# Three edits to the planned order of an attention and feed-forward kernel: a later load, six small transfers on another queue, exponentials ahead of casts

## The chip, the cores and the metric

The kernel runs on one core of one Trainium2 chip. The metric is the device time of one execution in microseconds; the median of three runs before the change is 892.74 us (892.28 to 894.45). The engines are TensorE (PE; its weight loads are listed as PEld), VectorE (DVE), ScalarE (ACT), GpSimd (POOL) and SyncE (SP), which here issues transfers only. Each works through its own instructions in order and waits on semaphores for the others. Transfers are issued from the queue of SyncE or of ScalarE.

## The reference, cut to what matters

Attention with a block mask over 4 batches x 8 heads, 768 positions, 64 dimensions a head, in float32, and then a feed-forward layer with the activation h - tanh(h):

```python
scores = q @ k.T / sqrt(64)                    # per batch and head, 768 x 768
scores = where(mask, scores, -1e9)             # blocks of 32: window, border, sampled
attn = exp(scores - scores.max(-1)); attn /= attn.sum(-1) + 1e-9
x = (attn @ v)                                 # heads side by side: 3072 tokens x 512
h = x @ w_in                                   # 512 -> 2048
out = (h - tanh(h)) @ w_out                    # 2048 -> 512
```

## The kernel before, in words

Heads are taken in 16 pairs. For a pair, `x` (its keys and queries, 768 KB), and `v` are loaded; VectorE splits `x` into high words and low rests in three pieces (`mask_words` into a PSUM bank, `low_words` into the tile `lo`), and SyncE copies high and low parts into one of three *slots*, from which TensorE reads its operands. A slot also holds 24 rows that add the mask, and one row, the 89th, that holds for each query the negated maximum of its scores.

That row is made per head `h` well ahead of use. TensorE computes the 88-row product (`smax`), VectorE takes maxima out of PSUM (`most`, tile `mc`), joins them (`most_join`, tile `mj`), TensorE turns them (`most_turn`), VectorE negates them into the tile `nm` (`most_send`), and a transfer of 3 KB puts `nm` into the slot's row 88. All matmuls of that head's scores (89 rows) wait for this transfer.

The scores are worked off in 96 *units* `n` (two key blocks of 128 rows, three units a head), each in three pieces of 512 columns, one PSUM bank each. `scores` fills the bank on TensorE, `exps` takes the exponential on ScalarE into the tile `pe`, `high` casts it to 16 bits in two halves (`ph`, ScalarE), `low` subtracts (`pl`, GpSimd up to unit 89), and `accum` multiplies both with the split `v` (tile `vhl`) on TensorE, 36 small matmuls a unit, into two banks of their own. The other six banks go round among scores, maxima and the small things by a counter (`bank`). Once in a pair ScalarE also casts `v` (`v_parts`, one or two instructions), in the first four pairs GpSimd subtracts for it too. In `low` and `v_parts` a name such as `pl` or `vhl` in a row of the profile is the tile written.

What sets the order is a list: `at(time, function, ...)` puts each step at a planned time, in units of half an attention unit (unit `n` stands at 2n), the list is sorted and every engine keeps that order. `smt(n)` is the planned time of unit n's maxima, 12 to 16 ahead of its scores. `LATE` shifts, for pairs 2 to 6, the load of `x`, its splitting and its copies to the slot (three numbers a pair). The loads of weights for the feed-forward part and its first conversions run within the attention; the feed-forward layer follows from about 350 us, on the same list. Since each recorded operation goes through one helper, nearly all rows of the profile bear its line, L91, and are told apart by tile names.

Of the kernel before, what the change touches and what calls it, by code (L numbers as in the profile page):

```python
# [64 lines left out]
TAIL, LASTN = 90, 93  # L65
SPIN = (-40, 14), (-1.95, 6), (-0.2, 2), (3.1, 3), (3.5, 1)
RAMP, NRAMP = 4, 24
LATE = {2: (10, 10, 6), 3: (8, 9, 3), 4: (5, 8, 2), 5: (2, 4, 1), 6: (1, 2, 0.5)}

THR2 = 0.16  # L70
C3 = -0.01988785306343693
# [33 lines left out]
@with_exitstack  # L105
def attention_ffn(ctx, tc, kq, v, samp, w_in, w_out, blocks, out):
    nc = tc.nc
    cst = ctx.enter_context(tc.tile_pool(name="cst", bufs=1))
    dpool = ctx.enter_context(tc.tile_pool(name="dpool", bufs=1, space=DRAM))
    xscr = [dpool.tile([P, T, DM], F32, name=f"xscr{b}") for b in range(B)]  # L110

    ident = cst.tile([P, P], F32, name="ident")
    make_identity(nc, ident)
    bias = [cst.tile([P, 1], F32, name=f"bias{i}") for i in range(2)]
    for x, val in zip(bias, (QB, THR2)):
        nc.vector.memset(x, val)

    slots = [cst.tile([P, 4, 2, S], F32R, name=f"slot{i}") for i in range(NSLOT)]
    wt = {(m, ft): dpool.tile([P, 512], F32, name=f"w{m}{ft}") for ft in range(NPRE) for m in "io"}
    part = [dpool.tile([P, DM], F32, name=f"part{j}") for j in range(CT)]  # L120
    f2 = ctx.enter_context(tc.tile_pool(name="f2", bufs=2))
    px = ctx.enter_context(tc.tile_pool(name="px", bufs=2))
    ffn = FFN(tc, w_in, w_out, xscr, ident, bias, slots, wt, out, f2, part, px)
    psum = ctx.enter_context(tc.tile_pool(name="psum", bufs=1, space=PSUM))
    banks = [psum.tile([P, 512], F32, name=f"ps{i}") for i in range(8)]
    ffn.banks, ffn.hb, ffn.cv, ffn.xt = banks[:4], banks[4:6], banks[6], banks[7]
    with ExitStack() as actx:
        turn = iter(range(10**6))
        ps = lambda n=6: banks[next(turn) % n], banks[6:]
        ffn.nc = InOrder(tc)  # L130
        attention(actx, tc, kq, v, samp, w_in, w_out, blocks, xscr, ident, ps, slots, wt, px, f2, ffn)
        ffn.nc = InOrder(tc, InOrder.ENGINES[:4])
    with ExitStack() as fctx:
        ffn.rest(fctx)


def attention(ctx, tc, kq, v, samp, w_in, w_out, blocks, xscr, ident, ps, slots, wt, px, f2, ffn):
    nc = InOrder(tc)
# [164 lines left out]
    mcs, sms = {}, {}  # L303
# [30 lines left out]
    def most_send(h):  # L334
        pr, j = divmod(h, 2)
        nm = p2.tile([T, P], F32R, tag="nm", name=f"nm{h}")
        nc.vector.tensor_scalar(out=nm, in0=mcs.pop(h), scalar1=-1.0, scalar2=8.0 * PBITS * math.log(2.0), op0=ALU.mult, op1=ALU.add)
        nc.sync.dma_start(
            out=sB[pr % NSLOT].bitcast(F32)[88:89, j, :].rearrange("o (t c) -> o t c", t=T), in_=nm.bitcast(F32)
        )  # L340

# [72 lines left out]
    def at(time, f, *args):  # L414
        ev.append((time, len(ev), f, args))
# [19 lines left out]
    for pr in range(NPAIR):  # L435
        t0 = 12 * pr
        late = LATE.get(pr, (0, 0, 0))
        at(t0 - 34.2 + late[0] if pr > 1 else -26.6 if pr else -49, load_x, pr)
# [27 lines left out]
    def smt(n):  # L466
        return 2 * n - LEAD + RAMP * max(0, 1 - n / NRAMP)

    for h in range(2 * NPAIR):
        t0 = smt(3 * h + 2)  # L470
        late = 0 if h < 4 else 0.8
        at(t0 + (2.65 if h > 4 else 1.6), most_join, h)
        at(t0 + 2.5 + late, most_turn, h)
        at(t0 + 2.75 + late, most_send, h)
        for step in range(3):
            at(6 * h + 10.3 + 0.5 * step, norm, h, step)
    for n in range(6 * NPAIR):
        for x in range(3):
            at(2 * n + 0.45 * x, scores, n, x)
            at(smt(n) + 0.45 * x + 0.25, smax, n, x)  # L480
            if n < 3:
                at(smt(n) + 0.45 * x + 0.26, spin, 1)
            at(smt(n) + 0.45 * x + 0.6, most, n, x)
            at(2 * n + 0.45 * x + 0.4, exps, n, x)
        at(2 * n + 1, high, n, 0)
        at(2 * n + 1.6, high, n, 1)
        at(2 * n + 1.7, low, n)
        at(2 * n + LAV, accum, n)
# [367 lines left out]
```

## Time and profile before

| | before |
|---|---|
| median of three runs | 892.74 us (892.28 to 894.45) |
| the profiled execution's own time | 895.38 us |
| its span, first to last instruction | 893.6 us |
| mean granted TensorE clock | 0.998 |
| TensorE busy | 875.4 us (98%) |
| VectorE busy | 717.8 us (80%) |
| ScalarE busy | 648.6 us (73%) |
| GpSimd busy | 505.8 us (57%) |

All durations come from the one profiled execution, so sums are made against its 895.38 us, which are 2.64 us above the median of the runs; 1.8 us of them lie outside the span. A row of a timeline gives start, duration, engine, line, operation, tile written <- tiles read, shapes and count, and in brackets the idle time before it and who ended that. A row of a stage gives the stretch, its length, the busy time of PE, PEld, DVE, ACT and POOL with their counts, the granted TensorE clock (1.00 is full), the share of time the 16 DMA engines were busy, and GB/s. TensorE's busy time is modelled for pipelined matmuls and can hide waits of some 0.1 us.

### The profile page before, as it was taken

The numbers are of one execution on the slowest core, as the hardware profiler recorded it, in microseconds if no ns is written. First come the engines' busy times: TensorE is split into PE (matmuls) and PEld (weight loads), VectorE is DVE, ScalarE is ACT, GpSimd is POOL, SyncE is SP. The second block draws the span as 40 slices with busy tenths as digits, with TensorE's granted clock in tenths as the row PEclk, the third lists the DMA queues.
The fourth block names the chain that finished last, engine by engine and source line by source line (L and its number), as shares of the span: only waits on it lengthen the run. The fifth ranks groups of instructions, "written<-read, shape, count | busy, mean of one in ns | idle before, by whom it ended". The sixth has DMA issues, their size and how long they took to land.

```text
span 893.6 us, 18523 instructions
## 1 busy us (share of the span) xinstructions
PE 875.4 (98%) x7078; PEld 734.8 (82%) x7078; DVE 717.8 (80%) x1262; ACT 648.6 (73%) x1080; POOL 505.8 (57%) x266
## 2 busy tenths in 40 slices
PE   7899999999999999999999999999999999999997
PEld 6778878888888888878888888888888888888885
DVE  8888899999999988998997687676668666866664
ACT  5799989999999999777776655565556555555553
POOL 7788989999999995677775222222222222222222
PEclk9999999999999999999999999999999999999999
DMA  6787788887888865347420202120102010001001
GB/s 182 191 212 182 182 218 206 204 210 193 211 214 222 199 173 175 117 142 225 140 76 34 63 7 66 30 34 15 47 5 34 10 47 1 1 1 48 0 1 47
DMA packets 87316, 97.53 MB, mean 109 GB/s; under 512 B 41764, under 2 KB 62436, under 8 KB 87228
## 3 DMA queue, kind: packets, MB, share of 16 engines
q1 hardware_dynamic: 86764, 95.31, 40.9%
q10 hardware_dynamic: 464, 1.05, 0.5%
q8 instruction: 55, 0.90, 0.4%
q14 instruction: 33, 0.27, 0.1%
HBM read 44.64 MB, written 15.20 MB: 67 GB/s over the span
## 4 chain that ended last, share of the span: by engine, by line
PE 80%; DVE 10%; DMA 5%; issue 2%; ACT 2%; POOL 1%; SPq 1%; ACTq 0%; DVEq 0%; POOLq 0%
PE ps L91 80%; DVE mc L91 4%; DVE ps L91 2%; DMA rawx<-kq 1%; DMA slot<-nm 1%; DVE lo L91 1%; DMA stage<-w_out 1%; DMA slot<-rawx 1%; ACT pe L91 1%; DMA rawv<-v 1%; SPq L91 1%; ACT ph L91 1%; DVE xq L91 1%; DVE pl L91 1%; DVE cvti L91 0%
## 5 line engine op out<-in xcount | busy, mean ns | idle before, releaser
L91 POOL TENSOR_TENSOR pl<-pe,ph 128x1536 f16<-128x1536 f32 x90 | 287.2, 3206 | 33.6 <-ACT ph L91 22.0
L91 POOL TENSOR_TENSOR gl<-t,gh 128x512 fp32r<-128x512 f32 x96 | 125.0, 1302 | 309.0 <-ACT gh L91 293.0
L91 PE MATMUL ps<-slot 128*128 128x512 f32 (+5 forms) x1224 | 257.7, 355 | 9.0 <-DMA slot<-nm 2.2
L91 PEld LDWEIGHTS ps<-slot 128*128 128x128 f32 (+2 forms) x1224 | 186.8, 191 | 38.0 <-DVE mc L91 4.1
L91 DVE TENSOR_REDUCE mc<-ps 128x1 f32<-128x512 f32 (+1 forms) x288 | 192.4, 680 | 21.4 <-PE ps L91 20.0
L91 ACT ACTIVATE u<-ps 128x512 f32<-128x512 f32 x96 | 57.4, 598 | 197.7 <-PE ps L91 197.7
L91 ACT ACTIVATE pe<-ps 128x512 f32<-128x512 f32 x288 | 164.0, 586 | 17.6 <-PE ps L91 14.4
L91 PE MATMUL ps<-slot,wx 128*128 128x512 f32 x720 | 173.0, 389 | 0.0
L91 ACT ACTIVATE ph<-pe 128x768 f16<-128x768 f32 x187 | 157.6, 843 | 5.4
L91 PEld LDWEIGHTS ps<-slot,wx 128*128 128x128 f32 x720 | 135.2, 188 | 28.0
L91 PE MATMUL ps<-wx,gh 128*128 128x512 f32 x480 | 147.9, 389 | 0.0
L91 PEld LDWEIGHTS <-ph 128*128 128x128 f16 x2304 | 112.6, 97 | 16.1 <-issue 13.1
L91 DVE TENSOR_TENSOR t<-t,ps 128x512 f32<-128x512 f32 x74 | 50.7, 685 | 88.1 <-ACT t L91 88.1
L91 PE MATMUL ps<-vhl,ph 128*128 128x65 f16 (+1 forms) x2304 | 120.6, 195 | 0.0
L91 PE MATMUL ps<-vhl,pl 128*128 128x65 f16 x1152 | 116.3, 193 | 0.6 <-DVE pl L91 0.3
L91 PEld LDWEIGHTS <-pl 128*128 128x128 f16 x1152 | 107.2, 100 | 1.0 <-POOL pl L91 0.6
L91 PEld LDWEIGHTS ps<-wx,gh 128*128 128x128 f32 x480 | 90.1, 188 | 18.5
L91 PE MATMUL ps<-wx,gl 128*128 128x512 f32 x240 | 93.5, 389 | 0.0
L91 DVE COPY_PREDICATED t<-mk,ps 128x512 f32<-128x512 int32 x96 | 71.3, 743 | 6.7 <-ACT mk L91 0.4
L91 DVE TENSOR_TENSOR ps<-ps,u 128x512 f32<-128x512 f32 x96 | 66.6, 694 | 11.5 <-ACT hs L91 11.4
L91 DVE SCALAR_TENSOR_TENSOR ps<-qq,ps 128x512 f32<-128x512 f32 x96 | 66.6, 694 | 8.0 <-DVE ps L91 0.5
L91 PE MATMUL ps<-slot,slot 128*128 128x512 f32 x288 | 69.6, 391 | 0.6 <-DVE t L91 0.6
(103 smaller groups left out, 1186.6 us busy)
## 6 DMA issues: line engine op xcount, KB each, us to landing
slot<-rawx SPq DMA_DIRECT2D x31, 384.0 KB, 7.1
slot<-lo SPq DMA_DIRECT2D x62, 192.0 KB, 3.1
slot<-rawx SPq DMA_DIRECT2D x61, 192.0 KB, 4.1
rawx<-kq SPq DMA_DIRECT2D x15, 768.0 KB, 6.1
stage<-w_in SPq DMA_DIRECT2D x13, 512.0 KB, 3.8
stage<-w_out SPq DMA_DIRECT2D x13, 512.0 KB, 4.0
rawv<-v SPq DMA_DIRECT2D x16, 384.0 KB, 5.3
xscr<-xq SPq DMA_DIRECT2D x16, 384.0 KB, 3.6
```

The costliest lines, as they stand in the source:

```text
L91: r = f(*args, **kw)
```

## The change

Three things move; nothing is computed differently.

The load of the third pair's `x` is planned 4.2 later (from -0.2 to 4.0) and its splitting 3 later. The 3 KB transfer of `nm` becomes a step of its own, `most_dma`; for the first six heads it is issued from ScalarE's queue, planned 0.3 after the negation, for the others from SyncE's as before. And for units 8 to 89 the first cast is planned at 2n + 1.35 instead of 2n + 1, which is after the third exponential (2n + 1.3).

```diff
-LATE = {2: (10, 10, 6), 3: (8, 9, 3), 4: (5, 8, 2), 5: (2, 4, 1), 6: (1, 2, 0.5)}
+APART = 8
+EARLYH = 6
+LATE = {2: (14.2, 13, 6), 3: (8, 9, 3), 4: (5, 8, 2), 5: (2, 4, 1), 6: (1, 2, 0.5)}
...
         nc.vector.tensor_scalar(out=nm, in0=mcs.pop(h), scalar1=-1.0, scalar2=8.0 * PBITS * math.log(2.0), op0=ALU.mult, op1=ALU.add)
-        nc.sync.dma_start(
+        mcs[h] = nm
+
+    def most_dma(h):
+        pr, j = divmod(h, 2)
+        nm = mcs.pop(h)
+        (nc.scalar if h < EARLYH else nc.sync).dma_start(
             out=sB[pr % NSLOT].bitcast(F32)[88:89, j, :].rearrange("o (t c) -> o t c", t=T), in_=nm.bitcast(F32)
         )
...
         at(t0 + 2.75 + late, most_send, h)
+        at(t0 + 2.75 + late + (0.3 if h < EARLYH else 0), most_dma, h)
...
-        at(2 * n + 1, high, n, 0)
+        at(2 * n + (1.35 if APART <= n < TAIL else 1), high, n, 0)
```

On ScalarE, from the last exponential of unit 1 into unit 2 (`pe1` is unit 1's exponentials, `ph1` its casts, `ps3` bank 3, the number behind `_` a running one), before:

```order
L91 ACTIVATE pe1_294<-ps3_98 128x512
L91 ACTIVATE ph1_309<-pe1_294 128x768
L91 ACTIVATE pe2_336<-ps2_97 128x512
L91 ACTIVATE pe2_336<-ps4_99 128x512
L91 ACTIVATE ph2_348<-pe2_336 128x768
L91 ACTIVATE pe2_336<-ps0_95 128x512
```

and now:

```order
L93 ACTIVATE pe1_292<-ps3_98 128x512
L93 ACTIVATE ph1_307<-pe1_292 128x768
L93 DMA slot0_73<-nm1_326 1x6x128
L93 ACTIVATE pe2_336<-ps2_97 128x512
L93 ACTIVATE pe2_336<-ps4_99 128x512
L93 ACTIVATE ph2_346<-pe2_336 128x768
L93 ACTIVATE pe2_336<-ps5_100 128x512
```

Head 1's transfer stands between unit 1's second cast and unit 2's first exponential, and unit 2's third exponential reads bank 5 instead of bank 0.

On ScalarE, units 9 and 10, with the two casts of the third pair's `v` (`rawv2`, `vhl2`) between, before:

```order
L91 ACTIVATE pe9_827<-ps1_96 128x512
L91 ACTIVATE pe9_827<-ps3_98 128x512
L91 ACTIVATE ph9_842<-pe9_827 128x768
L91 ACTIVATE pe9_827<-ps5_100 128x512
L91 ACTIVATE rawv2_474<-rawv2_474,sb2_812 128x768
L91 ACTIVATE vhl2_111<-rawv2_474 128x12x64
L91 ACTIVATE ph9_842<-pe9_827 128x768
```

and now:

```order
L93 ACTIVATE pe9_827<-ps1_96 128x512
L93 ACTIVATE pe9_827<-ps3_98 128x512
L93 ACTIVATE pe9_827<-ps5_100 128x512
L93 ACTIVATE ph9_883<-pe9_827 128x768
L93 ACTIVATE rawv2_472<-rawv2_472,sb2_812 128x768
L93 ACTIVATE vhl2_111<-rawv2_472 128x12x64
L93 ACTIVATE ph9_883<-pe9_827 128x768
```

The first cast went behind the third exponential; the casts of `v` still stand ahead of the second cast.

On SyncE, from the copies of the second pair's `x` on (`rawx1`, `rawv1` and `lo1` are of the second pair, `rawx2` of the third), before:

```order
L91 DMA slot1_74<-rawx1_173 64x768 x2
L91 DMA rawx2_245<-kq 128x1536
L91 DMA rawv1_270<-v 128x768
L91 DMA slot1_74<-rawx1_173 64x768 x2
L91 DMA slot1_74<-lo1_265 64x768
L91 DMA slot0_73<-nm1_328 1x6x128
L91 DMA slot1_74<-lo1_265 64x768 x3
L91 DMA rawv2_474<-v 128x768
L91 DMA slot2_75<-rawx2_245 64x2x768
L91 DMA slot1_74<-nm2_526 1x6x128
L91 DMA rawx3_538<-kq 128x1536
```

and now:

```order
L93 DMA slot1_74<-rawx1_173 64x768 x2
L93 DMA rawv1_268<-v 128x768
L93 DMA slot1_74<-rawx1_173 64x768 x2
L93 DMA slot1_74<-lo1_263 64x768
L93 DMA rawx2_328<-kq 128x1536
L93 DMA slot1_74<-lo1_263 64x768 x3
L93 DMA rawv2_472<-v 128x768
L93 DMA slot2_75<-rawx2_328 64x2x768
L93 DMA rawx3_536<-kq 128x1536
```

The third pair's `x` went behind the first low part of the second pair, the transfers of `nm1` and `nm2` are gone from this queue, and the load of the fourth pair's `x` follows the third pair's copy at once.

## The prediction, made before the changed kernel was run

> **What bounds the kernel now.** I read the page first, then the granted clock by stage, then TensorE's idle time and what ended it, then the queues that end it. The page:
>
> ```profile
> PE 875.4 (98%) x7078; PEld 734.8 (82%) x7078; DVE 717.8 (80%) x1262; ACT 648.6 (73%) x1080; POOL 505.8 (57%) x266
> ```
>
> TensorE is the bound, so only time in which it idles or runs slowly can be won. By stage (busy time of each engine, granted clock, DMA share):
>
> ```profile
> 29.89:33.30 3.41, 1.80 (x11) 1.29 (x10) 2.94 (x5) 0.59 (x3) 3.10 (x1) 1.00 1.04 235
> 33.30:36.71 3.41, 3.41 (x42) 2.89 (x41) 1.38 (x3) 2.71 (x5) 0.56 (x1) 0.50 0.78 171
> 36.71:40.12 3.41, 3.41 (x50) 3.02 (x49) 3.25 (x8) 2.46 (x5) 2.56 (x1) 1.00 0.00 0
> ```
> ```profile
> 200.00:250.00 50.00, 49.85 (x690) 43.10 (x689) 47.71 (x105) 48.45 (x75) 46.71 (x16) 1.00 0.80 206
> ```
>
> In the steady attention (200 to 250 us) TensorE idles 0.15 of 50 us: nothing to win, though ScalarE (48.45) and GpSimd (46.71) are nearly full too. The early stretch is different: of 3.41 us TensorE idles 1.6, and in the next 3.41 us it is granted half its clock, worth 3.41 x 0.5 = 1.7 us. TensorE's rows name the stall:
>
> ```profile
> 17.43 0.50 PE L91 MATMUL ps<-slot 89*128 89x512 f32 x1
> ...
> 27.70 0.95 PE L91 MATMUL ps<-slot 128*128 128x512 f32 x3 [0.91 <-DVE mc L91]
> ...
> 29.61 0.94 PE L91 MATMUL ps<-slot 88*128 88x256 f32 x4
> 32.16 2.02 PE L91 MATMUL ps<-slot 89*128 89x512 f32 x8 [1.61 <-DMA slot<-nm]
> ...
> 67.57 1.92 PE L91 MATMUL ps<-slot 89*128 89x512 f32 x9 [0.57 <-DMA slot<-nm]
> ```
>
> The 89-row matmul reads the row of negated maxima, so it waits until that 3 KB transfer lands. The chain of waits gives issue and flight:
>
> ```profile
> 27.08 5.04 DMA slot<-nm
> ```
> ```profile
> 61.53 6.00 DMA slot<-nm
> ```
>
> Head 0's transfer was fast: SyncE issued it at 15.46 and the matmul that needs it ran at 17.43, at most 1.97 us.
>
> ```profile
> 15.46 0.80 SPq L91 DMA_DIRECT2D slot<-nm x1
> ```
>
> So 5.04 and 6.00 us are about 2 us of transfer and 3 to 4 us behind the bulk loads on SyncE's queue (DMA share 1.04 in the row of 29.89 us).
>
> **The change, part by part.** (1) *Head 1's maxima on ScalarE's queue.* They are ready when VectorE's row ends, 26.78 + 0.27 = 27.05:
>
> ```profile
> 26.78 0.27 DVE L91 TENSOR_SCALAR nm<-ps 6x128 fp32r<-6x128 f32 x1
> 26.98 0.67 DVE L91 TENSOR_REDUCE mc<-ps 128x2 f32<-128x512 f32 x1
> ```
>
> In the new order the transfer stands between units 1 and 2 on ScalarE. Before, ScalarE ran there:
>
> ```profile
> 26.34 1.09 ACT L91 ACTIVATE pe<-ps 128x512 f32<-128x512 f32 x2
> ...
> 28.46 0.60 ACT L91 ACTIVATE pe<-ps 128x512 f32<-128x512 f32 x1 [0.17 <-PE ps L91]
> 29.09 0.84 ACT L91 ACTIVATE ph<-pe 128x768 f16<-128x768 f32 x1
> 32.75 1.08 ACT L91 ACTIVATE pe<-ps 128x512 f32<-128x512 f32 x2 [2.81 <-PE ps L91]
> ```
>
> ScalarE will wait for 27.05 and issue; taking 0.75 us per issue (head 0's issue is 0.80) it goes on at 27.83, 1.49 late. Behind it in its queue stand unit 2's exponentials and casts: 27.83 + (29.09 - 26.34 - 0.17) + 0.75 = 31.16 is when unit 3's first exponential can start, against 32.75 before. That is a gain of 1.6 on ScalarE's side; the 1.49 are covered by its 2.81 us of idle time.
>
> TensorE's side: the third x's first mask tile no longer takes a PSUM bank, so unit 2's third score tile moves from bank 0 (read by the maximum that ends at 26.98 + 0.67 = 27.65, the 0.91 us wait) to bank 5, free at 27.05. TensorE's work from 27.70 to 30.55 (29.61 + 0.94) then starts at about 27.1 and ends at 29.95. The transfer lands at 27.08 + 1.97 = 29.05 if its queue is what delayed it, at 27.08 + 5.04 = 32.12 if the DMA engines are. TensorE's gain is thus 32.16 - 29.95 = 2.2 at most, 0 at least. I take 1.6, ScalarE's, since the next units need its banks, and the fast landing because a 3 KB transfer alone on its queue is nearest to head 0's row.
>
> [...] No row here has a small transfer on ScalarE's queue beside loads.
>
> (2) *The half clock* follows the idle window; without the wait TensorE is busy through it. Worth 1.7 in the profiled execution (bounds 0 to 1.7). [...]
>
> (3) *Heads 2 to 5.* Heads 2 and 3 never delayed TensorE: 0. Each costs ScalarE 0 to 0.75 us of issuing; where the queue's issuing runs ahead of the engine it is 0, and I take 0. Head 4's landing (67.53) moves to about 63.5 and takes away the 0.57. Head 5 is ready at 73.40 and now stands ahead of the unit's third exponential, which ran at 73.53 and would be free to run at about 72.7 in the new order: it goes at 73.40 + 0.75 = 74.15, 0.6 late.
>
> ```profile
> 73.13 0.27 DVE L91 TENSOR_SCALAR nm<-ps 6x128 fp32r<-6x128 f32 x1
> ```
> ```profile
> 73.53 0.58 ACT L91 ACTIVATE pe<-ps 128x512 f32<-128x512 f32 x1
> ```
>
> Its second cast ends 1.25 late, GpSimd's subtraction behind it too. That one ends at 66.03 + 12.37 = 78.40 (the four rows from 66.03 quoted in (4)), and TensorE reads it at 80.61, so 2.2 us cover it: 0; uncovered 1.25.
>
> ```profile
> 80.61 0.19 PE L91 MATMUL ps<-vhl,pl 128*128 128x65 f16 x1
> ```
>
> (4) *Exponentials together, casts after* (units 8 to 89). An undisturbed unit before:
>
> ```profile
> 46.04 1.06 ACT L91 ACTIVATE pe<-ps 128x512 f32<-128x512 f32 x2
> 47.13 0.84 ACT L91 ACTIVATE ph<-pe 128x768 f16<-128x768 f32 x1
> 47.89 0.58 ACT L91 ACTIVATE pe<-ps 128x512 f32<-128x512 f32 x1
> 48.50 0.84 ACT L91 ACTIVATE ph<-pe 128x768 f16<-128x768 f32 x1
> 49.25 1.07 ACT L91 ACTIVATE pe<-ps 128x512 f32<-128x512 f32 x2
> ```
>
> It takes 3.21: exponential to exponential 0.48, exponential to the cast that needs it 0.61 (twice), cast to the next 0.75 (twice). In the new order each cast starts when its input has long been done: 3 x 0.48 + 2 x 0.75 = 2.94, so 0.27 less of ScalarE per unit. But the third exponential now needs TensorE's third score tile earlier. In a unit with the casts of v:
>
> ```profile
> 56.66 1.08 PE L91 MATMUL ps<-slot 88*128 88x512 f32 x3
> ```
> ```profile
> 57.48 0.84 ACT L91 ACTIVATE ph<-pe 128x768 f16<-128x768 f32 x1
> 58.23 0.58 ACT L91 ACTIVATE pe<-ps 128x512 f32<-128x512 f32 x1
> 58.71 0.93 ACT L91 ACTIVATE rawv<-rawv,sb 128x768 f32<-128x768 f32 x1
> ...
> 60.42 0.82 ACT L91 ACTIVATE ph<-pe 128x768 f16<-128x768 f32 x1
> ```
>
> The score is done at 57.74, so the third exponential starts at 57.83, ScalarE idles from 57.45, the first cast starts at 58.31, the casts of v at 59.06 and the second cast at 60.77 rather than 60.42: 0.35 late. What waits is GpSimd:
>
> ```profile
> 61.38 3.13 POOL L91 TENSOR_TENSOR pl<-pe,ph 128x1536 f16<-128x1536 f32 x1 [1.16 <-issue]
> 64.47 1.60 POOL L91 TENSOR_TENSOR vhl<-rawv,vhl 128x768 f16<-128x768 f32 x1
> 66.03 12.37 POOL L91 TENSOR_TENSOR pl<-pe,ph 128x1536 f16<-128x1536 f32 x4
> ```
> ```profile
> 69.41 0.19 PE L91 MATMUL ps<-vhl,pl 128*128 128x65 f16 x1
> ```
>
> GpSimd runs without a break from 61.38; the first of the four rows from 66.03 ends at about 69.15, 0.27 before TensorE reads it at 69.41. So a TensorE that comes there earlier by head 4's 0.57 and by the wait below waits for GpSimd instead: I keep 0.3 of the 0.57.
>
> ```profile
> 63.63 1.47 PE L91 MATMUL ps<-slot 128*128 128x256 f32 x7 [0.34 <-ACT pe L91]
> ```
>
> This wait goes (the third exponential runs 0.9 earlier). Near 92 us the same happens: TensorE already waits for GpSimd there, so what it gains before is waited for.
>
> ```profile
> 92.20 0.20 PE L91 MATMUL ps<-vhl,pl 128*128 128x65 f16 x1 [0.26 <-POOL pl L91]
> ```
>
>  For part 4 I take 0.3, bounds a gain of 1.5 (ScalarE never waited for) and a loss of 1.5 (0.35 on GpSimd's queue in a few places with under 0.3 us of room).
>
> (5) *Third x loaded later*: 768 KB leave the queue ahead of head 1's maxima, and later loads that stood behind heads 2 and 3 there can use the stretch from 36.71 in which the DMA engines stood still (share 0.00). VectorE's six mask steps, of 128 x 512 elements like the maximum of 0.67 us above, move with it to where it was busy 1.38 of 3.41 us (33.30) and later. 0, beside bank 5 in (1); uncovered, 4 us of VectorE in a stretch that is near full.
>
> *Sum*: against the profiled execution's own time, 895.38 - 1.6 - 1.7 - 0.3 - 0.3 = 891.5. That execution is 2.64 above the median of the runs; 1.7 of these I hold to be the half clock, which the median run then has not. So against the median 892.74 - 1.6 - 0.3 - 0.3 = **890.5**.
>
> **The rivals.** (A) *The half clock was in the median too.* Then the whole 1.7 comes on top: 888.8. For it: the window with 1.80 of 3.41 us busy lies in every run; against: the spread of the three runs. (B) *The wait only changes queues.* Head 1's transfer lands at 32.1 on ScalarE's queue as well, since the DMA share is 1.04 there; ScalarE's 1.49 hide in its 2.81. Left are 0.3 + 0.3: 892.1. (C) *Slower: the second cast comes too late.* In each of some 14 pairs from unit 8 on, the unit with v's casts ends later and GpSimd hands that on. In the steady part:
>
> ```profile
> 211.85 10.02 POOL L91 TENSOR_TENSOR pl<-pe,ph 128x1536 f16<-128x1536 f32 x3 [1.13 <-ACT ph L91]
> ```
> ```profile
> 222.91 0.19 PE L91 MATMUL ps<-vhl,pl 128*128 128x65 f16 x1
> ```
>
> GpSimd's third result is there at 221.87, 1.0 before TensorE reads it. At my 0.35 that room holds. If ScalarE's wait for the third score makes it 1.4, each of 14 pairs loses 0.4: 890.5 + 5.6 = 896.1. For it: GpSimd's 46.71 of 50. Against: a late ScalarE no longer waits, and then gains its 0.27 per unit. That the new order does nothing at all in the steady part is in the forecast already.
>
> **How the numbers follow.** Forecast 0.48, A 0.27, B 0.17, C 0.08. About 0.3% (2.7 us) is what a measurement here can tell from no change: below 890.06 is faster, above 895.4 slower. A is faster, and the forecast, with 0.8 of spread either way, about three times in ten: 0.27 + 0.14 = 0.41. C is slower: 0.08. Same is 0.51. Range: 888.3 (A with 0.5 more) to 892.8 (B with the bound of parts 3 and 4).
>
> **What would show it.** Right: head 1's 89-row matmul near 30 us without a wait on the maxima, no half clock after it, ScalarE waiting near 26.5 to 27.8 us, units of 2.9 us where ScalarE lags, and waits on GpSimd's result near 69 and 92 us. Wrong: a wait of over 1 us for the maxima at 30 us (B); waits on GpSimd's result in most pairs after 100 us (C); a time under 889 (A, or waits behind ScalarE that I held to be hidden).

## The result, and the profile after

The changed kernel takes 902.99 us (median; 900.48 to 905.34), the kernel before 892.51 in the same comparison: a ratio of 1.0113, interval 1.0090 to 1.0136. The forecast was 890.5, the range 888.3 to 892.8: the change makes it about 10 us slower, on a side to which the prediction gave a chance of 0.08, and the time lies beyond even the slower rival's 896.1.

The changed kernel's profiled execution took 904.7 us. Its page says nothing of the cause, because TensorE's share hardly moves:

```profile
PE 877.6 (97%) x7078; PEld 735.2 (81%) x7078; DVE 719.7 (80%) x1262; ACT 642.2 (71%) x1080; POOL 506.3 (56%) x266
```

What TensorE waited for does (the view of waits of the changed kernel: us in total, times, the longest):

```profile
PE ps L93 <- DMA slot<-nm: 8.2, 3, 5.0
PE ps L93 <- DVE slot L93: 2.0, 1, 2.0
...
PE ps L93 <- POOL pl L93: 1.5, 2, 0.9
```

`slot<-nm` is the transfer of the negated maxima, the very one that was to become faster. Before, TensorE waited for it 2.2 us in all, in the profile on which the prediction rests. The three waits are those of heads 0, 1 and 2. The chain of waits of the changed kernel gives issue and flight of each:

```profile
17.21 5.47 DMA slot<-nm
...
33.41 3.64 DMA slot<-nm
...
43.75 7.46 DMA slot<-nm
```

Head 0's flight was 1.97 us at most before. Around it, the changed kernel's timeline (start, duration, engine; SPq and ACTq are the issuing instructions of SyncE and ScalarE):

```profile
14.61 4.29 SPq L93 DMA_DIRECT2D slot<-rawx  x4
15.16 0.27 DVE L93 TENSOR_SCALAR nm<-ps 6x128 fp32r<-6x128 f32 x1
17.21 1.26 ACTq L93 DMA_DIRECT2D slot<-nm  x1
...
22.72 2.50 PE L93 MATMUL ps<-slot 89*128 89x512 f32 x8 [4.99 <-DMA slot<-nm]
```

The first row matters most. Before, SyncE issued these four slot copies (384 and 192 KB) from 16.30 on, *after* head 0's maxima at 15.46; now from 14.61 on, before the maxima exist. And the stages (busy time of each engine, granted clock, DMA share):

```profile
17.26:22.72 5.46, 0.47 (x2) 0.16 (x2) 1.22 (x3) 0.00 (x0) 1.98 (x3) 0.58 1.02 232
22.72:27.60 4.88, 4.88 (x17) 4.30 (x18) 2.87 (x5) 3.07 (x5) 0.00 (x0) 0.50 0.40 101
...
51.25:55.00 3.75, 3.75 (x28) 3.05 (x29) 2.07 (x3) 2.96 (x5) 3.75 (x2) 0.63 0.02 5
```

While TensorE idles the 16 DMA engines are full (1.02). Then the work comes at half clock: 4.88 x 0.50 = 2.4 us lost in the second row, and 3.75 x 0.37 = 1.4 after head 2's wait. The half clock goes on a little beyond these rows, to 28.34 and to 55.65 us, which makes it some 4.5 us in all.

A second profile of the kernel before (891.72 us, span 889.9, shown with its experiment) waited 1.1 us for the maxima. Against it the span is 13.0 longer. Counted by TensorE's matmuls (7078 in each profile), the changed kernel is 11.1 us behind at 100 us. The waits for the maxima (8.2 - 1.1 = 7.1) and the half clock (some 4.5) account for that, to half a microsecond. The other 1.9 us come between 100 and 300 us and are not taken apart here; two profiles of the kernel before differ by 1.2 in that stretch. The longer wait for `DVE slot` (2.0 against 1.1) costs nothing: the matmul behind it starts at 8.22 us in both profiles.

### The profile page after: what moved, and what is told of

Its sections match the earlier page's. It is cut to its first block, busy times and chain, and to the rows that moved or that the text cites. A ratio compares the mean times of both kernels' runs of the same rounds, so it can differ in the third digit from the quotient of the medians.

```text
span 902.9 us, 18525 instructions
## 1 busy us (share of the span) xinstructions
PE 877.6 (97%) x7078; PEld 735.2 (81%) x7078; DVE 719.7 (80%) x1262; ACT 642.2 (71%) x1080; POOL 506.3 (56%) x266
## 4 chain that ended last, share of the span: by engine, by line
PE 80%; DVE 9%; DMA 4%; issue 2%; ACT 2%; SPq 1%; POOL 1%; ACTq 0%; DVEq 0%; POOLq 0%
PE ps L93 80%; DVE mc L93 3%; DVE ps L93 2%; DMA slot<-nm 2%; DVE pl L93 1%; SPq L93 1%; DMA slot<-lo 1%; DMA rawv<-v 1%; DMA slot<-rawx 1%; ACT pe L93 1%; DMA rawx<-kq 0%; DVE xq L93 0%; DVE lo L93 0%; ACT ph L93 0%; DVE cvti L93 0%
## 5 line engine op out<-in xcount | busy, mean ns | idle before, releaser
L93 PE MATMUL ps<-slot 128*128 128x512 f32 (+5 forms) x1224 | 260.6, 357 | 13.9 <-DMA slot<-nm 8.2
L93 ACT ACTIVATE pe<-ps 128x512 f32<-128x512 f32 x288 | 165.9, 597 | 37.7 <-PE ps L93 25.3
L93 ACT ACTIVATE ph<-pe 128x768 f16<-128x768 f32 x187 | 149.7, 840 | 0.7
```

Source lines behind the costliest of these rows:

```text
L93: r = f(*args, **kw)
```

## The experiments

**Theory:** SyncE's wait for the maxima had been holding back the bulk copies behind it in its order. With the wait moved to ScalarE, SyncE issues them early, the 3 KB then travel among them, TensorE idles and falls to half clock. **Rivals:** the later load of the third x did it; ScalarE's new unit order did it; a small transfer on ScalarE's queue is slow by itself.

### One part alone: the maxima on ScalarE's queue

```diff
-LATE = {2: (14.2, 13, 6), ...
+LATE = {2: (10, 10, 6), ...
-APART = 8
+APART = 90
```

> The first six rows of maxima go out on ScalarE's queue; the third pair's x is loaded where it was before, and ScalarE's units have their old order. Theory (SyncE, no longer held by the wait for the maxima, issues its bulk copies early; the 3 KB transfer then waits among them, TensorE idles and falls to half clock): the whole loss is there, 900 to 904 us, with a wait of 4 to 6 us for head 0's maxima near 22 us and a clock near 0.5 just before it. Rival 1 (the later load of the third pair's x is the cause): 891 to 895. Rival 2 (the order of ScalarE's units is the cause): 891 to 895.

Measured: 903.51 us, ratio 1.0138 (1.0121 to 1.0154). Two long flights stand in its chain; TensorE waited 4.8 and 2.9 us for them:

```profile
17.30 5.28 DMA slot<-nm
...
43.69 7.18 DMA slot<-nm
```

This part alone loses as much as the whole change (10.9 and 10.5 us); it needs neither of the other two parts for that.

### The other two parts without it

```diff
-EARLYH = 6
+EARLYH = 0
```

> The changed kernel with all rows of maxima back on SyncE's queue: the later load and the new order of ScalarE's units remain. Theory: 890 to 894 us, head 0's maxima used about 2 us after they are issued, no half clock before 30 us. Rivals 1 and 2 (later load, or order of the units): 900 or more.

Measured: 896.02 us, ratio 1.0032 (1.0016 to 1.0049). No 5 us wait, no half clock before 30 us; but 3.4 us over the kernel before, which neither the theory (890 to 894) nor the rivals (900 or more) had expected; two later experiments take these parts one by one. Its timeline serves below as the reference for head 1:

```profile
27.24 0.75 SPq L93 DMA_DIRECT2D slot<-nm  x1
28.04 0.42 SPq L93 DMA_DIRECT2D rawx<-kq  x1
28.51 1.80 SPq L93 DMA_DIRECT2D slot<-lo  x3
```
```profile
29.87 0.78 PEld L93 LDWEIGHTS ps<-slot 89*128 89x128 f32 x4
```

The 89-row weights load at 29.87 without a wait: on SyncE's queue, with 768 KB and three copies issued right *behind* them, head 1's maxima were there within 2.6 us.

### SyncE held as before, the transfer still on ScalarE's queue

```diff
 def most_send(h):
     ...
+    if h < EARLYH:
+        nc.sync.dma_start(out=hold[h], in_=nm.bitcast(F32))
```

> The changed kernel, with six transfers of 3 KB added: SyncE copies each of the first six rows of maxima to a scratch place in DRAM, at the place in its order where it sent them before. So SyncE is held by the same wait as before, while the transfer that TensorE needs still goes by ScalarE's queue. Theory (SyncE set free is the cause): 890 to 895 us, head 0's maxima used about 2 us after issue on ScalarE's queue. Rival 3 (a small transfer on ScalarE's queue is slow beside loads, whatever SyncE does): head 0's wait near 22 us stays at 4 to 5 us, 899 or more.

Measured: 901.68 us, ratio 1.0103 (1.0089 to 1.0117). Head 0's wait fell from 4.99 to 0.42 us, but head 1's grew:

```profile
27.88 0.29 SPq L93 DMA_DIRECT2D hold<-nm  x1
27.88 0.70 ACTq L93 DMA_DIRECT2D slot<-nm  x1
28.22 0.33 SPq L93 DMA_DIRECT2D rawx<-kq  x1
28.60 1.75 SPq L93 DMA_DIRECT2D slot<-lo  x3
...
33.65 2.93 PE L93 MATMUL ps<-slot 89*128 89x512 f32 x8 [2.74 <-DMA slot<-nm]
```

The theory in its first form falls: it expected 890 to 895. Heads 0 and 2 bear it out: held back, SyncE left head 0 a wait of 0.42 us and head 2 none, where ScalarE's queue, if it were slow whatever SyncE does, should have kept head 0's wait at 4 to 5 us. Heads 1 and 4 do not. Head 4 waited 2.91 us, but SyncE was not held there: it had copied the maxima to scratch at 64.13 and gone on, and ScalarE, busy with its own work, issued them at 65.60. For head 1 the same bulk was issued in the same order as in the experiment before, *behind* the maxima, and 2.6 us became 5.7. Two things at least differ: the queue, and the lead over the load, which is 0.34 us here (27.88 and 28.22) and was 0.80 (27.24 and 28.04).

The DMA packets of this trace show more (`q1` is SyncE's queue, `q10` ScalarE's; packets, MB and share of the engines' time). First from 27.8 to 31.5 us, where `q10` has none; then from 31.5 to 32.8; then, around head 2's maxima, from 42.8 to 43.3, where `q1` has none:

```profile
q1 hardware_dynamic: 98, 0.53, 62.5%
```
```profile
q10 hardware_dynamic: 12, 0.00, 1.0%
```
```profile
q10 hardware_dynamic: 12, 0.00, 3.0%
```

Head 1's maxima, 12 small packets, went only when 86 of the load's 128 packets had run. SyncE's own copy of the same 3 KB, issued at 27.88 as well, is the 12 other packets of the first row, and ran from 28.63 to 28.72, ahead of the load. Head 2's maxima had the same lead over a load of the same size:

```profile
41.81 0.68 ACTq L93 DMA_DIRECT2D slot<-nm  x1
42.15 0.33 SPq L93 DMA_DIRECT2D rawx<-kq  x1
```

Their first packet ran at 43.12, 1.31 us after issue, and the load's first at 43.38. For head 1 the load's first packet ran at 29.20, 0.98 us after its issue; 1.31 us after 27.88 is 29.19. So a lead of 0.34 us on another queue is just about none: once the 3 KB came before the load, once among it. Whether ScalarE's queue does as well as SyncE's with a lead of 0.80, no run here shows.

### Head 1 only

```diff
-(nc.scalar if h < EARLYH else nc.sync).dma_start(
+(nc.scalar if h in (1,) else nc.sync).dma_start(
```

> The changed kernel, but of the maxima only head 1's go by ScalarE's queue. The prediction's first step by itself, with parts A and C: by the step 1.6 us under the kernel with A and C alone, and no wait for head 1's maxima near 30 us. Theory of SyncE set free: the slot copies behind head 1's maxima go out early and the transfer shares the engines with them, so a wait of 0.5 to 2 us near 30 to 32 us remains and the time is within 1 us of the kernel with A and C alone, 890 to 894.

Measured: 897.30 us, ratio 1.0061 (1.0044 to 1.0078), 1.3 above the two other parts without it, though the two intervals overlap. Both the step (1.6 below those two parts) and the theory (890 to 894, a wait of up to 2 us) had expected less. This is the prediction's first step by itself:

```profile
24.17 0.77 SPq L93 DMA_DIRECT2D rawx<-kq  x1
26.94 1.90 SPq L93 DMA_DIRECT2D slot<-lo  x3
27.13 1.29 ACTq L93 DMA_DIRECT2D slot<-nm  x1
...
33.00 2.93 PE L93 MATMUL ps<-slot 89*128 89x512 f32 x8 [2.84 <-DMA slot<-nm]
```

5.8 us instead of the 1.97 that the step took. Here SyncE, no longer held at 27.1, has put the third x (24.17) and a copy (26.94) in front. The wait of 2.84 is larger than the one that was to be removed, and the two other parts without this one have no such wait.

### SyncE held until the transfer has landed

The theory in its second form: what delays the 3 KB on ScalarE's queue is bulk that SyncE issues ahead of them *or up to a few us behind them*. The copy to scratch now reads the place where the maxima land.

```diff
 def most_dma(h):
     row = sB[...][88:89, j, :] ...
     (nc.scalar if h < EARLYH else nc.sync).dma_start(out=row, in_=nm.bitcast(F32))
+    if h < EARLYH:
+        nc.sync.dma_start(out=hold[h]..., in_=row)
-at(t0 + 2.75 + late + (0.3 if h < EARLYH else 0), most_dma, h)
+at(t0 + 2.75 + late, most_dma, h)
```

> The changed kernel, but SyncE copies each of the first six rows of maxima to scratch from the place where they land, not from where they start: it holds its later bulk loads back until the transfer on ScalarE's queue has landed. (Added: six transfers of 3 KB; the 0.3 by which those six transfers were planned later is left out, so that SyncE's order is that of the held kernel.) Theory A, from the held kernel (a small transfer on ScalarE's queue waits for bulk that SyncE issues beside or behind it): heads 0 and 1 land about 2 to 3 us after issue, their waits (0.42 and 2.74 us in the held kernel) go under 0.5 and 1, and the time falls to 893 to 898. Theory B (ScalarE's queue is slow by itself): the wait of over 2 us for head 1 stays and the time is 901 or more, since SyncE's loads come later too.

Measured: 898.79 us, ratio 1.0070 (1.0057 to 1.0083), 0.8 above the range of theory A. Head 0 is used 2.2 us after issue, head 1 at 30.02, 2.75 after:

```profile
27.27 0.70 ACTq L93 DMA_DIRECT2D slot<-nm  x1
...
30.02 1.25 PEld L93 LDWEIGHTS ps<-slot 89*128 89x128 f32 x8 [0.17 <-DMA slot<-nm]
30.04 0.25 SPq L93 DMA_DIRECT2D hold<-slot  x1
30.34 0.33 SPq L93 DMA_DIRECT2D rawx<-kq  x1
```
```profile
38.87 0.38 PE L93 MATMUL ps<-ident,mj 128*6 128x128 f32 x1 [3.71 <-DVE lo L93]
```

ScalarE's queue is therefore not slow by itself: theory A's point. The place of the bulk decides it: the queue is the same as in the held kernel, and so is the order of the loads, yet head 1 took 5.7 us there and 2.75 here. What this kernel loses instead stands in the last row: the third x is late (its load issued at 30.34 rather than 28.04), VectorE's mask step with it, and TensorE waits 3.71 us for that.

### Head 0 alone, head 2 alone

```diff
-(nc.scalar if h < EARLYH else nc.sync).dma_start(
+(nc.scalar if h in (0,) else nc.sync).dma_start(
```

Both are made from the kernel before, with its loads and its unit order; the second has `(2,)`.

> The kernel before, with only head 0's maxima on ScalarE's queue. If head 0 carries the first wait and the half clock after it (5.0 us of wait, 10 us at half clock in the changed kernel's profile): 896 to 900, with a wait of over 4 us near 22 us. If the loss needs the later heads too: under 895. The prediction did not price head 0 at all.

> The kernel before, with only head 2's maxima on ScalarE's queue. If a small transfer there waits for the bulk loads that SyncE is free to issue: a wait of 2 to 3 us for it near 45 to 50 us and 894 to 897. If head 2's wait in the changed kernel came only from the lateness that head 0 had caused: no wait, 892 to 893. The prediction's step: 0.

Measured: head 0 alone 897.91 us, ratio 1.0059 (1.0046 to 1.0072); head 2 alone 896.88, ratio 1.0042 (1.0028 to 1.0057). Head 0's timeline, and then head 2's chain:

```profile
14.73 4.23 SPq L93 DMA_DIRECT2D slot<-rawx  x4
...
16.88 1.39 ACTq L93 DMA_DIRECT2D slot<-nm  x1
...
21.92 2.50 PE L93 MATMUL ps<-slot 89*128 89x512 f32 x8 [4.53 <-DMA slot<-nm]
```
```profile
38.34 6.98 DMA slot<-nm
```

For head 2, what SyncE issues now and what TensorE waits for:

```profile
31.14 0.60 SPq L93 DMA_DIRECT2D rawx<-kq  x1
...
45.36 2.25 PE L93 MATMUL ps<-slot 89*128 89x512 f32 x11 [2.91 <-DMA slot<-nm]
```

Before, SyncE issued that load at 39.95, right after head 2's maxima at 39.16. Both results fall where the theory put them. Head 0 costs 5.0 us and head 2 4.4, without any lateness that another head caused; together that is 9.4 of the 10.9 us that the six cost, if the two simply add, which no run shows.

### The later load alone, the unit order alone

```diff
# the later load alone
-EARLYH = 6
-APART = 8
+EARLYH = 0
+APART = 90
# the unit order alone
-LATE = {2: (14.2, 13, 6), ...
-EARLYH = 6
+LATE = {2: (10, 10, 6), ...
+EARLYH = 0
```

> Only ScalarE's unit order is new; x and the maxima are as before. The later load and this order together cost 3.4 us in the run before this. If the order of the units costs it (second cast late, GpSimd behind): 895 to 897. If the later load costs it: 892 to 893. The prediction's step for this part: 0.3 us faster, 892.3.

> Only the third pair's x is loaded later; the maxima are on SyncE's queue, the units in the old order. If the later load costs the 3.4 us: 895 to 897. If the order of the units does: 892 to 893, or 1 to 2 us faster, since head 1's maxima no longer stand behind 768 KB (in the profile of the kernel with both, TensorE's wait for them was gone). The prediction's step for this part: 0.

Measured: the unit order alone 894.38 us, ratio 1.0022 (1.0014 to 1.0031); the later load alone 893.81, ratio 1.0006 (0.9997 to 1.0015). Both lie between the ranges that their expectations named. The unit order costs 1.5 us by the medians, 1.2 to 2.8 by the interval. Over the stretch from 100 to 390 us, the kernel before (its second profile) and then the unit order alone (PE, PEld, DVE, ACT, POOL busy):

```profile
100.00:390.00 290.00, 287.92 (x3842) 247.91 (x3842) 273.05 (x543) 274.41 (x434) 253.50 (x92) 1.00 0.74 194
```
```profile
100.00:390.00 290.00, 287.23 (x3834) 245.71 (x3832) 272.29 (x542) 267.07 (x430) 253.10 (x90) 1.00 0.74 193
```

ScalarE is busy 7.3 us less, as intended, and TensorE gets through no more matmuls for it. Weight loads that waited for an exponential, from 100 to 360 us (the same two profiles):

```profile
PEld ps L91 <- ACT pe L91: 2.2, 6, 0.5
```
```profile
PEld ps L93 <- ACT pe L93: 5.0, 12, 0.5
```

Such waits double, from 6 to 12; the two profiles of both parts together have 13 and 12 of them, the first profile of the kernel before 5. That is where I would look for the 1.5 us; it is a reading of profiles and not an experiment. The waits on GpSimd that rival C foresaw in most pairs do not occur: from 100 to 360 us TensorE has none in this profile.

The later load alone does what it says to head 1, whose wait is gone, and gives it back near 36 us, where TensorE waits for a mask step of the x that now comes later:

```profile
36.32 0.27 PE L93 MATMUL ps<-ident,mj 128*6 128x128 f32 x1 [1.12 <-DVE lo L93]
```

### Second profiles: the kernel before, and the later load with the unit order

Nothing is edited.

> The kernel before, for a second profile: the first one's execution took 895.38 us, 2.6 more than the median of its runs. The prediction held 1.7 of these to be the half clock at 33 to 37 us, which the median run has not. If so: about 892.5, with the wait of 1.6 us for head 1's maxima but the clock at full speed after it. If the half clock belongs to every run: the same 0.50 there and the difference lies elsewhere. If the wait itself varies: under 892.5 to 893 with no wait for head 1.

> The kernel with the later load and the new unit order once more, for a second profile: its first profile was its fastest run (893.5, median 896.0, highest 898.6). If the spread comes from the early stage (waits for the maxima, half clock), a run of 895 or more shows a wait of 1 us or more or a clock under 0.95 before 80 us; if it comes from the unit order, TensorE's idle time after 100 us is over the 1.6 us of the first profile by as much as the time is higher.

Measured: the kernel before at 891.72 us; the two parts at 895.05. The kernel before, in the same two slices as in the prediction and at head 1:

```profile
29.89:33.30 3.41, 2.89 (x32) 2.08 (x30) 2.94 (x5) 1.63 (x4) 3.12 (x1) 1.00 0.99 273
33.30:36.71 3.41, 3.41 (x42) 2.84 (x39) 3.38 (x8) 3.34 (x6) 1.49 (x1) 1.00 0.55 124
```
```profile
31.23 1.69 PE L91 MATMUL ps<-slot 89*128 89x512 f32 x8 [0.52 <-DMA slot<-nm]
```

There is no half clock, and the wait for head 1 is 0.52 us: neither the 1.61 nor the none at all that the expectation named. The prize for which the change was priced was thus mostly a trait of one of the two executions.

The second profile of the two parts took 1.55 us more than the first. Part of that is one place in the early stage (first, then second profile):

```profile
35.90 0.27 PE L93 MATMUL ps<-ident,mj 128*6 128x128 f32 x1 [0.88 <-DVE lo L93]
```
```profile
36.70 0.27 PE L93 MATMUL ps<-ident,mj 128*6 128x128 f32 x1 [1.52 <-DVE lo L93]
```

The same matmul runs 0.80 us later, 0.64 of it by this wait. Counted by matmuls, the second profile is still 0.8 behind at 150 us, 1.4 at 200 and 1.5 at the end. So neither alternative holds purely, and why the two parts together cost 3.4 us, when 1.5 and 0.9 were measured apart, stays open: the two intervals allow for it, the profiles do not show it.

### A version that might beat both

The later load alone, its mask steps planned 1 later.

```diff
-LATE = {2: (14.2, 13, 6), ...
+LATE = {2: (14.2, 14, 6), ...
```

> The later load of the third pair's x alone, as in the run that had only this, with its mask steps planned 1 later still (14 for 13). There, TensorE's waits for head 1's and head 4's maxima were gone (0.52 and 0.54 us in the second profile of the kernel before), but it waited 1.12 us near 36 us for VectorE's last mask step of that x. If this wait is what eats the gain: it goes, and the time is 0.5 to 1 us under the kernel before. If the gain is lost elsewhere, or the wait only moves: within 1 us of the kernel before, on either side.

Measured: 892.70 us against 892.87, ratio 0.9993 (0.9978 to 1.0007). The wait near 36 us is gone and another has come in, for head 4's maxima:

```profile
65.74 0.50 PE L93 MATMUL ps<-slot 89*128 89x512 f32 x1 [1.17 <-DMA slot<-nm]
```

No version here is measurably faster than the kernel before.

## Why the prediction was wrong, by its steps

**Step 1, head 1's maxima: the short flight did not come.** The step took 1.97 us of flight "because a 3 KB transfer alone on its queue is nearest to head 0's row". That row was of SyncE's queue, on which SyncE, having waited itself, issued its bulk from 16.30 on, 0.84 us behind the maxima. On ScalarE's queue head 1 took 3.64 us in the changed kernel, 5.8 and 5.7 with head 1 alone and with SyncE held, and 2.75 only when SyncE's bulk was kept back until it had landed. The worst bound, a landing after 5.04 us "if the DMA engines are" what delays it, was not a bound either: it assumed that what stood in the engines stays the same when the transfer leaves SyncE's queue. So the sum had no loss in it. The prize was also too large: 0.52 us in the second profile, not 1.61.

The held kernel shows how far off the short flight was: of the same 3 KB issued at the same moment (27.88 us), the packets on SyncE's queue had run by 28.72 us and those on ScalarE's ran from 31.54 on, after 86 of the load's 128 packets. The second queue was worse there and not only no better.

**Step 3, heads 2 to 5: the step that failed most, by what it left out.** Head 0 was moved as well, and was used only as the example of a fast transfer; its move was never priced. It costs 5.0 us alone. Head 2, priced at 0 because it "never delayed TensorE", costs 4.4 alone. Both were fast *because* SyncE was standing at their wait, with the bulk behind it; with SyncE held there again, they waited 0.42 us and not at all. The prediction named what is queued behind a waiting instruction on ScalarE, where the wait came, and not what had been queued behind it on SyncE, where the wait went.

**Step 2, the half clock: right, and then the wrong way round.** That the median execution before has none was an estimate, from one profile and the times of three runs; the second profile (891.72 us) shows 1.00 there, and rival A falls with it. But the changed kernel's profile has new ones, behind its waits for heads 0 and 2 (0.50 from 18.10 to 28.34 us and from 52.23 to 55.65), which cost some 4.5 us. A term for a half clock that is *gained* was missing.

**Step 4, the unit order: wrong in sign.** Taken as a gain of 0.3, bounds 1.5 either way; measured as a loss of 1.5 us (ratio 1.0014 to 1.0031, that is 1.2 to 2.8 us), at the edge of the bounds or beyond. ScalarE's saving is there and is worth nothing, since TensorE is the bound; the prediction's own first paragraph said as much of the steady part.

**Step 5, the later load: right.** 0 was taken; 0.9 us was measured, not to be told from none. The mechanism behind it, a wait removed at head 1 and one gained at a mask step, was half in the text ("move with it to where it was busy"), without a price.

**The rivals.** A: no; the window "with 1.80 of 3.41 us busy" that it took to lie in every run has 2.89 in the second profile. B ("the wait only changes queues"): the right place, but it priced the same lateness on another queue, where the lateness grew and spread to the heads that had none. C, the slower one: its mechanism does not appear, and the loss came from elsewhere.

## What to carry to other kernels

When a wait is taken off an in-order queue that also issues bulk loads, write down what stood behind it: from then on that work runs before, or beside, what the wait was for (here four slot copies, issued at 14.61 us instead of 16.30, and a flight of 5.47 us instead of 1.97 at most). A small transfer that is needed soon did best here on the *same* queue ahead of the bulk (2.0 to 2.6 us). Behind bulk on that queue it took 4.0 to 6.0 (heads 1 and 4 of the kernel before, two profiles), and on a queue of its own, beside bulk on another, 2.8 to 7.5 where TensorE waited for it. And price every instance that an edit moves, the one that is already fast first.

## What the runs showed of the hardware that I had not expected

**On a second queue, issuing first did not always mean going first.** In the held kernel the maxima of heads 1 and 2 were both issued 0.34 us ahead of a load of 768 KB on the other queue. The first packet of one ran 3.66 us after issue, among the load's, that of the other 1.31 us after, before them.

**Head 0's transfer was issued 1.78 us after its maxima were ready.** They were ready at 15.43 in the changed kernel, yet ScalarE, without other work from 13.84 on, issued them at 17.21. Two more kernels show the like: issue at 17.21, 17.30 and 16.88 (changed kernel, the maxima's part alone, head 0 alone), and TensorE's own wait for `slot<-lo` ended at 17.26, 17.35 and 16.93, 0.05 us later each time. That the issue waited for the landing of one of these slot copies is my reading of the times. In the two kernels with SyncE held it did not: ScalarE issued at 15.46, while TensorE waited for `slot<-lo` until 17.35 and 17.07. This is about 1.8 of the 5.3 us by which head 0's matmul comes later (22.72 against 17.43); how long the transfer would have flown from 15.46 on, with the copies issued at 14.61, no run here shows.

**The length of an idle spell alone did not decide on the half clock.** The unit order alone had it from 17.52 us on, after a wait of 1.04 us that ended at 17.16 (its stages):

```profile
14.11:17.52 3.41, 1.84 (x11) 1.33 (x10) 2.60 (x6) 0.00 (x0) 3.41 (x5) 1.00 0.54 160
17.52:20.93 3.41, 3.32 (x13) 2.92 (x13) 2.79 (x6) 1.66 (x3) 1.73 (x3) 0.50 0.99 214
```

The later load alone waited 1.02 us at the same place, until 17.14, and its clock was 1.00 from 17 to 41 us. Its stage at that wait:

```profile
13.68:17.09 3.41, 1.91 (x14) 1.45 (x12) 2.77 (x7) 0.17 (x1) 3.41 (x6) 1.00 0.70 227
```

The last kernel waited 1.3 us for `slot<-lo`, and its mean clock over the whole span was 0.999, as that of the later load alone, against 0.995 of the unit order alone. What decides between them, no run here shows.
